# The head of a linear-attention and Mish kernel laid out anew, three q chunks loaded in runs of eight rows, first states built in column tiles

## The chip, the cores and the metric

The kernel runs on one core of one Trainium2 chip. The metric is the device time of one execution in microseconds (us), lower is better; it is taken as the median of several runs. A profile is one further execution, recorded by the hardware profiler; its own time is given beside the runs.

The core has five engines with a queue each: PE (TensorE, matrix products; PEld are its weight loads), DVE (VectorE), ACT (ScalarE), POOL (GpSimd) and SP (SyncE, here used for DMA transposes). Each engine takes its instructions in the order in which the program issues them. Matrix products read the on-chip memory SBUF and write the accumulator memory PSUM, which DVE and ACT read.

## What is computed

Two stages with nothing between them but a change of layout. The first is a decaying linear attention, 4 batches, 8 heads, 768 positions, head size 64; the second is a matrix product, an activation h · tanh(softplus(h)) (called Mish on the chip) and a second matrix product, on the 3072 tokens of width 512 that the first stage gives.

```python
def _attn_ref(q, k, v, lam):                      # q, k, v: (4, 8, 768, 64)
    ...
    Dmask = np.where(rel >= 0, lam[:, None, None] ** rel[None, :, :], 0.0)
    lam_pow = lam[:, None, None] ** (pos[None, :, None] + 1)
    lam_block = lam ** block
    for b in range(nb):
        ...
        intra = np.einsum('bhic,bhjc->bhij', qb, kb) * Dmask[None]
        intra = np.einsum('bhij,bhjd->bhid', intra, vb)
        inter = np.einsum('bhid,bhde->bhie', qb * lam_pow[None], kv_state)
        out[:, :, sl] = intra + inter
        kb_dec = kb * rev_pow[None]
        kv_state = lam_block[None, :, None, None] * kv_state + np.einsum('bhsd,bhse->bhde', kb_dec, vb)
    return out

def _moe_ref(x, w_in, w_out):                     # (3072, 512), (512, 2048), (2048, 512)
    h = x @ w_in
    sp = np.where(h > 20.0, h, np.log1p(np.exp(np.minimum(h, 20.0))))
    g = h * np.tanh(sp)
    return (g @ w_out)
```

## The kernel before

**Tiling.** The 768 positions are cut into six groups n of 128 positions (the kernel uses blocks of 128, not the reference's 64). A chunk i = 4n + b is group n of batch b, with all 8 heads: 128 positions by 512. Group n has 4 chunks, thus 512 tokens.

**A chunk of groups 0 and 1** goes through three functions. `first_t` turns k and q on PE so that the head size lies on the partitions (four 128x128 transposes each, into the PSUM tiles `pk` and `pq`); ACT copies `pk` to `pkT` and DVE copies `pq` to `pqT`. `first_s` multiplies the two, eight products into two PSUM tiles `pS`, and DVE multiplies these with the decay table `dm` (group 0) or a triangle (group 1) into `sb`, two operations of 128x512. `first_o` multiplies `sb` with v into `pO`, eight products, for group 1 with four more that bring in the state of group 0; ACT copies `pO` to the chunk's columns of `xt`. Below, t(c), s(c) and o(c) stand for these three on chunk c.

**The second stage** takes `xt`. For group 0, `mm1_unit` u = 0 to 15 makes 128 of the 2048 hidden columns for all 512 tokens (four products of 512 columns into `ph`, of which there are two PSUM buffers) and ACT applies Mish into `hsg`. `mm1_part` does the first 384 tokens of such a unit ahead, when the fourth chunk is not there yet. For group 1, `mm1_tile` (c, s) makes a quarter of the hidden columns for one chunk (16 products of 128 columns). After that `mm2_unit` multiplies `hsg` with `w_out` (four products of 512 columns); from there on the steps of the attention for groups 2 to 5 (`pair_s`, `pair_o`, `pair_a`) are slipped in between the dense units at numbered places.

**The head** is the stretch until the units of group 0 run without a stop. PE also gets products of zeros there (`busy(m)`: m products of 512 columns), whose results nobody reads. The decays come from lam: its logarithm is spread over the partitions, and from it come `dm`, `lk`, `lq`, `lbc` and `lqt` by exponentials on ACT.

**States.** `state_step(0, b)` makes batch b's state after group 0: four 128x128 products of `ktil` (k scaled by `lk`, made by `scale_k`) with v into a PSUM tile `pv`, of which only the 64x64 blocks on the diagonal are wanted; DVE multiplies with `lbm`, which holds the decay there and zero elsewhere, into `w`. `state_step(1, b)` adds `w` on DVE and scales on POOL into `wcp`, eight small POOL operations in all. `group_state` does the same for later groups, with products of 64 columns into two halves of the partitions (column tiles), two chunks to a PSUM tile.

**What sets the order.** The schedule is written by hand: every engine runs its instructions in the order of the source. POOL is at once an engine and the queue that issues nearly all loads, also in source order: k, q and v of a chunk in 128 partitions times 8 heads of 256 bytes, the weights in rows of up to 2 KB. A load on POOL can wait for a free semaphore, that is for the load eight places before it to land; what stands behind it on POOL waits too. SP issues the DMA transposes of the later groups (`turn`: `qraw` and `kraw`), each after POOL has scaled the chunk's k.

## Time and profile before

| | us |
|---|---|
| three runs, median (lowest to highest) | 212.15 (211.38 to 212.17) |
| the profiled execution, its own time | 213.28 |
| its span, first to last instruction | 211.5 |
| PE / DVE / ACT / POOL busy in it | 203.1 / 69.3 / 86.3 / 102.4 |

The profiled execution took 1.1 us more than the median; 1.8 us of its time lie outside the span. Times in the views count from the start of the span. A row of the timeline merges neighbouring instructions of one kind: start, time until the last of them has ended, engine, line, what is written and read, how many, and in brackets how long the engine had been idle and what ended that. A product's end includes its way through the array, so the next row of PE can start before the row's end; the step from start to start tells how fast PE goes on.

### The profile page before, as it was taken

The page shows a single profiled execution, that of the slowest core. Times are in us where ns is not written, and L with a number is a line of the kernel's source. Part 1 is how long each engine was busy: PE and PEld are TensorE (multiplying, and loading weights), DVE is VectorE, ACT ScalarE, POOL GpSimd, SP SyncE. Part 2 cuts the span into 40 slices and gives each one's busy share as a digit, 9 for nine tenths or more (in the row PEclk, how much of TensorE's full clock was granted, in tenths as well). Part 3 has the DMA queues.
Part 4 walks back from the last instruction along what each step waited for, and adds up shares of the span by engine and source line. Part 5 has one row for each costly group of instructions (what it writes and reads, how often), then busy time and mean ns, then how long its engine had stood idle before and what let it go on. Part 6 is the DMA issues. An engine that isn't in the chain of part 4 may idle for free.

```text
span 211.5 us, 4241 instructions
## 1 busy us (share of the span) xinstructions
PE 203.1 (96%) x1728; PEld 110.2 (52%) x1728; DVE 69.3 (33%) x131; ACT 86.3 (41%) x146; POOL 102.4 (48%) x149
## 2 busy tenths in 40 slices
PE   7798999999997999999999999999999999999994
PEld 2465546999644544455544454544445544444442
DVE  6867746650004442042440042582042600000000
ACT  5664566656321111356412356312456221566120
POOL 7997379948992558796965076931000000000000
PEclk9999999999999999999999999999999999999999
DMA  9999999999999999999996999996902032100112
GB/s 132 132 159 172 192 145 115 152 195 168 114 146 209 195 179 177 171 188 148 149 161 152 190 81 84 144 167 152 183 1 51 3 99 99 51 3 0 50 50 99
DMA packets 109894, 26.76 MB, mean 127 GB/s; under 512 B 102578, under 2 KB 106930, under 8 KB 109874
## 3 DMA queue, kind: packets, MB, share of 16 engines
q0 software_dynamic: 78080, 13.37, 91.8%
q1 hardware_dynamic: 27296, 6.63, 20.4%
q10 hardware_dynamic: 4498, 6.49, 9.9%
q8 instruction: 13, 0.21, 0.5%
q14 instruction: 7, 0.06, 0.1%
HBM read 27.26 MB, written 6.29 MB: 159 GB/s over the span
## 4 chain that ended last, share of the span: by engine, by line
PE 75%; POOL 13%; DMA 9%; issue 1%; DVE 0%; POOLq 0%
PE po L431 35%; PE ph L399 27%; DMA kn<-in_k_dram 6%; PE ph L417 5%; DMA kraw<-ktil 3%; POOL vz L79 3%; POOL ktil L266 3%; POOL qn L76 2%; POOL kn L68 2%; PE pS L343 2%; PE pO L370 2%; POOL win L92 1%; POOL win L95 1%; PE pv L319 1%; PE pO L349 1%
## 5 line engine op out<-in xcount | busy, mean ns | idle before, releaser
L431 PE MATMUL po<-wout,hsg 128*128 128x512 f16 (+2 forms) x400 | 85.4, 371 | 0.0
L399 PE MATMUL ph<-xt,win 128*128 128x512 f16 (+2 forms) x332 | 73.5, 371 | 0.4 <-ACT hsg L406 0.2
L406 ACT ACTIVATE hsg<-ph 128x512 f16<-128x512 f32 x80 | 47.5, 597 | 30.2 <-PE ph L399 29.8
L431 PEld LDWEIGHTS <-hsg 128*128 128x128 f16 x400 | 37.8, 98 | 42.3
L399 PEld LDWEIGHTS <-win 128*128 128x128 f16 x332 | 30.9, 98 | 34.7 <-issue 1.5
L446 ACT ACTIVATE osb<-po 128x512 f32<-128x512 f32 (+1 forms) x24 | 14.2, 593 | 75.4 <-PE po L431 70.6
L358 DVE TENSOR_TENSOR sb<-pS,maskT 128x512 f16<-128x512 f32 x32 | 20.0, 683 | 64.0 <-PE pS L343 64.0
L68 POOL DMA_DIRECT2D kn<-in_k_dram x23 | 20.9, 909 | 5.3 <-issue 1.9
L79 POOL DMA_DIRECT2D vz<-in_v_dram x24 | 21.6, 905 | 2.7 <-DMA win<-in_moe_w_in_dram 2.0
...
L266 POOL TENSOR_TENSOR ktil<-kn,lk 128x512 f16<-128x512 f16 x16 | 16.6, 1050 | 3.0 <-ACT hsg L406 2.9
L376 DVE TENSOR_TENSOR xtok<-pO,lqt 128x512 f16<-128x512 f32 x16 | 10.3, 686 | 16.8 <-PE pO L370 16.8
L417 PE MATMUL ph<-xt,win 128*128 128x128 f16 x256 | 15.3, 219 | 0.0
L417 PEld LDWEIGHTS <-win 128*128 128x128 f16 x256 | 14.5, 98 | 0.1
L440 DVE COPY osb<-po 128x128 f32<-128x128 f32 x1 | 0.3, 290 | 38.7 <-PE po L431 38.7
L421 ACT ACTIVATE hsg<-ph 128x512 f16<-128x512 f32 x16 | 9.6, 597 | 6.9 <-PE ph L417 6.9
L387 POOL COPY tick<-hsg 1x1 f16<-1x1 f16 x25 | 4.4, 176 | 12.2 <-ACT hsg L406 12.1
L324 POOL TENSOR_TENSOR wc<-raws,lbc 128x512 f16<-128x512 f32 x6 | 6.6, 1113 | 5.5 <-DVE raws L323 5.5
L163 PE MATMUL busy<-kzero 128*128 128x512 f16 x18 | 7.6, 516 | 1.2 <-DVE kzero L149 1.2
L266 DVE TENSOR_TENSOR ktil<-kn,lk 128x512 f16<-128x512 f16 (+1 forms) x8 | 6.6, 846 | 0.0
L241 DVE TENSOR_TENSOR sb<-pS,maskT 128x512 f16<-128x512 f32 x8 | 5.2, 686 | 4.2 <-PE pS L237 4.2
L343 PE MATMUL pS<-qraw,kraw 64*128 64x128 f16 x128 | 5.1, 218 | 1.2 <-DMA kraw<-ktil 1.2
...
## 6 DMA issues: line engine op xcount, KB each, us to landing
...
```

Of the source, the lines that this page charges most:

```text
L68: nc.gpsimd.dma_start(out=kn[i], in_=chunk_rows(k, i))
L76: nc.gpsimd.dma_start(out=qn[i], in_=chunk_rows(q, i))
L79: nc.gpsimd.dma_start(out=vz[i % NVB][:, :, 0:D], in_=chunk_rows(v, i))
L266: (nc.vector if i < B or i >= (NG - 1) * B else nc.gpsimd).tensor_tensor(out=t, in0=kn[i], in1=bc(lk, 2, D), op=ALU.mult)
L358: nc.vector.tensor_tensor(out=s.sb[x][t], in0=pS[x][t], in1=bc(maskT, 1, JP), op=ALU.mult)
L376: nc.vector.tensor_tensor(out=xtok[:, :, :, t, :], in0=s.pO[t], in1=bc(bc(lqj[:, :, t], 1, 2), 3, D), op=ALU.mult)
L399: nc.tensor.matmul(ph_t[ni][:, lo:hi], win_t(ni, kc), xt[n][:, kc, lo:hi], start=(kc == 0), stop=(kc == NKC - 1))
L406: nc.scalar.activation(hsg[n][:, ni, :], ph_t.pop(ni), AF.Mish)
L417: nc.tensor.matmul(ph[:, u, :], win_t(w * s + u, kc), xt[n][:, kc, b * C : (b + 1) * C], start=(kc == 0), stop=(kc == NKC - 1),)
L421: nc.scalar.activation(hsg[n][:, w * s : w * s + w, b * C : (b + 1) * C], ph, AF.Mish)
L431: nc.tensor.matmul(po[:, lo:hi], hsg[n][:, ki, b * C : (b + 1) * C], wout[part][:, kk, lo:hi], start=(ki == 0), stop=(ki == NKI - 1),)
L446: nc.scalar.activation(o, i, AF.Copy)
```

## The change

- **q of chunks 1 to 3** is loaded with eight neighbouring positions of one head to a partition: 128 runs of 2 KB in place of 1024 runs of 256 bytes, into tiles of their own. Their turn on PE is 16 ordinary products with parts of the identity as the moving operand (64 columns each, into one or the other half of the partitions of a PSUM tile in f32) in place of four transposes into f16.
- **States of groups 0 and 1** come from `state_half`, the form in column tiles that later groups had: 16 products of 64 columns for two chunks. Group 0's go straight into the diagonal blocks of one tile `wst`, which DVE has cleared beforehand, by two DVE operations on 64 partitions each; `lbm` and its making are gone. Group 1's sum needs two DVE operations and one of POOL for each half. Group 0's are made after units 1 and 3 (before: after units 3, 5, 7 and 9), group 1's after tiles (6,1) and (6,2) (before: between (4,1) and (5,0)).
- **Decays.** The logarithm for pairs of heads (`lnp`) comes from two small products of its own instead of copies; `lq` from four ACT operations instead of one on DVE and one on ACT. Both halves of `dm`'s arguments are made before q of chunk 0 is cast.
- **Zero products.** Two stand between the turns of k and q of chunk 0; in all 16 in place of 18.
- **The end of the head.** s(3) now stands before o(2), and only units 0 and 1 have a part made ahead (before: units 0, 1 and 2). `scale_k(1)` is done before the units, `scale_k(2)` and `scale_k(3)` after unit 1.
- **Group 1's steps** each lie later among the units and tiles: t(4) after unit 12 (11), s(4) after 14 (13), t(5) and o(4) after 15, then tile (4,0) directly.
- **POOL's queue.** `scale_k(6)` stands ahead of the load of v of chunk 7.
- **The first pair steps** among the dense units of groups 0 and 1 stand at 11, 14 and 17 in place of 9, 13 and 16.

At the end of the head, PE's queue was this before (L217 the turn of chunk 3's q, L256 its o(2), L163 a zero product, L237 s(3), L399 the part of unit 0; a row for the weights and one for the product, repeats left out):

```order
L217 LDWEIGHTS qn
L217 MATMUL pq<-ident,qn 128x128
...
L256 LDWEIGHTS vz_71
L256 MATMUL pO<-sb,vz_71 128x128
...
L163 LDWEIGHTS kzero
L163 MATMUL busy<-kzero 128x512
L237 LDWEIGHTS pkT
L237 MATMUL pS<-pqT,pkT 128x128
...
L399 LDWEIGHTS win_77
L399 MATMUL ph<-xt,win_77 128x384
```

It is this now (L225 the new turn of q, L252 s(3), L271 o(2), L176 a zero product, L398 the part of unit 0):

```order
L225 LDWEIGHTS qn_119
L225 MATMUL pq<-ident,qn_119 64x64
L252 LDWEIGHTS pkT
L252 MATMUL pS<-pqT,pkT 128x128
...
L271 LDWEIGHTS vz_71
L271 MATMUL pO<-sb,vz_71 128x128
...
L176 LDWEIGHTS kzero
L176 MATMUL busy<-kzero 128x512
...
L398 LDWEIGHTS win_77
L398 MATMUL ph<-xt,win_77 128x384
```

o(2) moved behind s(3); the part of unit 0, which reads what o(2) gives, stays behind both.

DVE's queue around the first states, before (L266 scales k, L299 makes the state of one batch in two operations):

```order
L266 TENSOR_TENSOR ktil<-kn,lk 128x512
L299 TENSOR_TENSOR w_158<-pv,lbm 128x256
L299 TENSOR_TENSOR w_159<-pv,lbm 128x256
L266 TENSOR_TENSOR ktil<-kn,lk 128x512
L299 TENSOR_TENSOR w_160<-pv,lbm 128x256
L299 TENSOR_TENSOR w_161<-pv,lbm 128x256
```

And now (L281 scales k, L313 makes the state of two batches in two operations, one for each half of the partitions):

```order
L281 TENSOR_TENSOR ktil<-kn_98,lk 128x512
L281 TENSOR_TENSOR ktil<-kn,lk 128x512
L313 TENSOR_TENSOR wst<-pv,lbc 64x8x64 x2
L281 TENSOR_TENSOR ktil<-kn,lk 128x512 x2
L313 TENSOR_TENSOR wst<-pv,lbc 64x8x64 x2
```

The scaling of k of chunks 2 and 3 now stands behind the first half's states, one after the other.

PE's queue ahead of the first tile of group 1, before (L256 the last products of o(4), L237 s(5), L217 t(6), L417 tile (4,0)):

```order
L256 LDWEIGHTS vz_73
L256 MATMUL pO<-sb,vz_73 128x128
L237 LDWEIGHTS pkT
L237 MATMUL pS<-pqT,pkT 128x128
...
L217 LDWEIGHTS qn
L217 MATMUL pq<-ident,qn 128x128
L417 LDWEIGHTS win_77
L417 MATMUL ph<-xt,win_77 128x128
```

And now (L267 and L271 o(4), L416 tile (4,0)):

```order
L267 LDWEIGHTS wst
L267 MATMUL pO<-pqT,wst 128x128
L271 LDWEIGHTS vz_73
L271 MATMUL pO<-sb,vz_73 128x128
...
L416 LDWEIGHTS win_77
L416 MATMUL ph<-xt,win_77 128x128
```

s(5) and t(6) no longer stand between o(4) and the tile that reads its result.

The diff, cut to its core:

```diff
+        if i < B:
+            qn[i] = const.tile([128, RS, D], F16, name=f"qn{i}")
+            n, b = divmod(i, B)
+            nc.gpsimd.dma_start(
+                out=qn[i].rearrange("p r c -> p (r c)"),
+                in_=q[b, :, n * C : (n + 1) * C, :].rearrange("h (s r) c -> h s (r c)", r=RS))
...
+    half = const.tile([1, 2, 128], F32, name="half")
+    nc.vector.memset(half, 0.0)
+    for t in range(2):
+        nc.vector.memset(half[:, t, 64 * t : 64 * t + 64], 1.0)
...
     nc.tensor.matmul(lamb, one1, lam1, start=True, stop=True)
-    busy(3)
+    lamp = ps.tile([128, JP], F32, name="lamp", tag="pS")
+    for t in range(2):
+        nc.tensor.matmul(lamp, half[:, t, :], lam1.rearrange("p (j t) -> p j t", t=2)[:, :, t],
+                         start=(t == 0), stop=(t == 1))
+    busy(1)
...
     def q_decays():
-        nc.scalar.activation(lq, lq, AF.Exp)
-        nc.scalar.activation(lqt, lnb, AF.Exp, scale=eq)
-
-
-    lbm = const.tile([128, JP, 128], F32, name="lbm")
-
+        for j in range(JP):
+            nc.scalar.activation(lq[:, j, :], ei, AF.Exp, scale=lnp[:, j : j + 1])
+
+    own = ident.rearrange("p (j x s) -> p j x s", j=JP, x=2)
...
-    def first_t(c):
+    def first_t(c, m=0):
 
         out_ = []
         first = c < B
         for src, name in ((k0 if c == 0 else kn[c] if first else ktil[c], "pk"),
                           (q0 if c == 0 else qn[c], "pq")):
-            pt = ps.tile([128, JP, C], F16, name=name, tag=name)
-            for j in range(JP):
-                nc.tensor.matmul(
-                    pt[:, j, :], src[:, 2 * j : 2 * j + 2, :].rearrange("p h c -> p (h c)"), ident,
-                    is_transpose=True, start=(j == 0), stop=(j == JP - 1),
-                )
+            if 0 < c < B and name == "pq":
+                pt = ps.tile([128, JP, C], F32, name=name, tag=name)
+                for r in range(RS):
+                    for x in range(2):
+                        nc.tensor.matmul(
+                            pt[64 * x : 64 * x + 64].rearrange("p j (s r) -> p j s r", r=RS)[:, :, :, r],
+                            src[:, r, :], own[:, :, x, :], start=True, stop=True)
+            else:
+                pt = ps.tile([128, JP, C], F16, name=name, tag=name)
+                for j in range(JP):
+                    nc.tensor.matmul(
+                        pt[:, j, :], src[:, 2 * j : 2 * j + 2, :].rearrange("p h c -> p (h c)"), ident,
+                        is_transpose=True, start=(j == 0), stop=(j == JP - 1),
+                    )
             out_.append(work.tile([128, JP, C], F16, name=f"{name}T", tag=f"{name}T", bufs=2))
             if name == "pk":
                 nc.scalar.activation(out_[-1], pt, AF.Copy)
+                busy(m)
...
-    def state_step(n, b, spare):
-
-        i = n * B + b
-        pv = ps.tile([128, JP, 128], F32, name="pv", tag=spare, bufs=2)
-        for j in range(JP):
-            nc.tensor.matmul(
-                pv[:, j, :].rearrange("p (a e) -> p a e", a=2),
-                ktil[i][:, 2 * j : 2 * j + 2, :].rearrange("p h c -> p (h c)"),
-                vz[i % NVB][:, 2 * j : 2 * j + 2, 0:D], start=True, stop=True,
-            )
-        if n:
-            raw = work.tile([128, JP, 128], F32, name="raw", tag="raw", bufs=4)
-        for hf in range(2):
-            hs = slice(2 * hf, 2 * hf + 2)
-            if n == 0:
+    def state_half(n, h, spare, bufs=2):
+
+        pv = ps.tile([128, 2, JP, D], F32, name="pv", tag=spare, bufs=bufs)
+        for x in range(2):
+            i = n * B + 2 * h + x
+            for j in range(JP):
+                for t in range(2):
+                    nc.tensor.matmul(
+                        pv[64 * t : 64 * t + 64, x, j, :], ktil[i][:, 2 * j + t, :],
+                        vz[i % NVB][:, 2 * j + t, 0:D], start=True, stop=True)
+        rows = [slice(64 * t, 64 * t + 64) for t in range(2)]
+        own = [wst[rs, 2 * h : 2 * h + 2, :, rs] for rs in rows]
+        if n == 0:
+            for rs, o in zip(rows, own):
                 nc.vector.tensor_tensor(
-                    out=wst[b][hf], in0=pv[:, hs, :], in1=lbm[:, hs, :], op=ALU.mult)
-            else:
-                nc.vector.tensor_tensor(
-                    out=raw[:, hs, :], in0=pv[:, hs, :], in1=wst[b][hf], op=ALU.add)
-        if n:
-            for t in range(2):
-                rs = slice(64 * t, 64 * t + 64)
-                nc.gpsimd.tensor_tensor(
-                    out=wcp[b // 2][0][rs, b % 2, :, :], in0=raw[rs, :, rs],
-                    in1=bc(lbc[rs, :], 2, D), op=ALU.mult)
-
...
+                    out=o, in0=pv[rs], in1=bc(bc(lbc[rs, :], 1, 2), 3, D), op=ALU.mult)
+            return
+        raw = work.tile([128, 2, JP, D], F32, name="raws", tag="raws", bufs=2)
+        if n == 1:
+            for rs, o in zip(rows, own):
+                nc.vector.tensor_tensor(out=raw[rs], in0=pv[rs], in1=o, op=ALU.add)
+        else:
             nc.vector.tensor_tensor(out=raw, in0=pv, in1=wcp[h][n % 2], op=ALU.add)
-            nc.gpsimd.tensor_tensor(
-                out=wcp[h][(n + 1) % 2], in0=raw, in1=bc(bc(lbc, 1, 2), 3, D), op=ALU.mult)
+        nc.gpsimd.tensor_tensor(
+            out=wcp[h][(n + 1) % 2], in0=raw, in1=bc(bc(lbc, 1, 2), 3, D), op=ALU.mult)
 
     def pair_a(s):
         if s.n < NG - 1:
-            group_state(s.n, s.spare)
+            for h in range(2):
+                state_half(s.n, h, s.spare)
...
+    def clear(b):
+        nc.vector.memset(wst[:, b], 0.0)
+
     nc.scalar.activation(k0, kn[0], AF.Copy)
+    nc.scalar.activation(lnp, lamp, AF.Ln)
     decays(0)
-    pair_decays()
+    decays(1)
     nc.vector.tensor_copy(q0, qn[0])
     nc.scalar.activation(dm[:, 0], dm[:, 0], AF.Exp)
-    decays(1)
-    first_t(0)
+    first_t(0, 2)
+    clear(0)
     nc.scalar.activation(dm[:, 1], dm[:, 1], AF.Exp)
-    q_arguments()
+    nc.scalar.activation(lk, lnb, AF.Exp, scale=ek)
+    nc.scalar.activation(lqt, lnb, AF.Exp, scale=eq)
+    nc.scalar.activation(lbc, lnp, AF.Exp, scale=float(C))
     busy(1)
     first_s(0)
-    nc.scalar.activation(lk, lnb, AF.Exp, scale=ek)
-    nc.scalar.activation(lbc, lnp, AF.Exp, scale=float(C))
+    first_t(1)
+    clear(1)
     q_decays()
-    busy(2)
-    first_t(1)
-    nc.scalar.preload_act_table(AF.Mish)
     busy(1)
+    first_o(0)
     first_s(1)
-    first_o(0)
     busy(3)
     first_t(2)
-    busy(1)
+    clear(2)
+    nc.scalar.preload_act_table(AF.Mish)
+    first_o(1)
     first_s(2)
-    first_o(1)
     busy(3)
     first_t(3)
+    clear(3)
+    first_s(3)
     first_o(2)
-    busy(1)
-    first_s(3)
+    busy(2)
     mm1_part(0, 0, 0, GT - C)
     first_o(3)
     mm1_part(0, 1, 0, GT - C)
-    mm1_part(0, 2, 0, GT - C)
     scale_k(0)
-    nc.vector.memset(lbm, 0.0)
-    for hp in range(2):
-        rs = slice(64 * hp, 64 * hp + 64)
-        nc.vector.tensor_copy(lbm[rs, :, rs], bc(lbc[rs, :], 2, D))
+    scale_k(1)
...
     scale_k(B + 1)
     load_q(NVB - 1)
+    scale_k(B + 2)
     load_v(NVB - 1)
...
-    steps = {11: ((first_t, 4),), 13: ((first_s, 4),), 14: ((first_t, 5),),
-             15: ((first_o, 4), (first_s, 5), (first_t, 6))}
+    steps = {12: ((first_t, 4),), 14: ((first_s, 4),), 15: ((first_t, 5), (first_o, 4))}
     for u in range(NKI):
         mm1_unit(0, u)
-        if u in (3, 5, 7, 9):
-            state_step(0, (u - 3) // 2, "po")
-        if u in (1, 3, 5):
-            scale_k((u + 1) // 2)
+        if u in (1, 3):
+            state_half(0, u // 2, "po")
+        if u == 1:
+            scale_k(2)
+            scale_k(3)
...
-    steps = {(4, 0): ((first_o, 5), (first_s, 6)), (4, 1): ((first_t, 7), (state_step, 0)),
-             (4, 2): ((first_o, 6), (first_s, 7), (state_step, 1)), (4, 3): ((state_step, 2),),
-             (5, 0): ((first_o, 7), (state_step, 3))}
+    steps = {(4, 0): ((first_s, 5), (first_t, 6)), (4, 1): ((first_o, 5), (first_s, 6)),
+             (4, 2): ((first_t, 7),), (4, 3): ((first_o, 6), (first_s, 7)), (5, 0): ((first_o, 7),),
+             (6, 1): ((state_half, 0),), (6, 2): ((state_half, 1),)}
     for c in range(B, 2 * B):
         for s in range(WS):
             mm1_tile(c, s)
             for f, i in steps.get((c, s), ()):
-                f(*((1, i, "po") if f is state_step else (i,)))
+                f(*((1, i, "po") if f is state_half else (i,)))
...
-            steps = (((9, pair_s, 0), (13, pair_o, 0), (16, pair_s, 1), (20, pair_o, 1),
+            steps = (((11, pair_s, 0), (14, pair_o, 0), (17, pair_s, 1), (20, pair_o, 1),
                       (24, pair_a, 1)) if n < NT else
```

29 lines of the change are left out of this document (6 added, 23 removed).

## The prediction

> **What bounds the kernel.** I read the page's busy times and chain first, then the timeline of the first 25 us, then the rows at which PE stands still.
>
> ```profile
> PE 203.1 (96%) x1728; PEld 110.2 (52%) x1728; DVE 69.3 (33%) x131; ACT 86.3 (41%) x146; POOL 102.4 (48%) x149
> PE 75%; POOL 13%; DMA 9%; issue 1%; DVE 0%; POOLq 0%
> ```
>
> PE is busy 203.1 of 211.5 us and carries 75% of the chain. Whatever delays PE anywhere stays to the end; whatever leaves PE alone is worth nothing. PE has room in the head and at a few waits. The head:
>
> ```profile
> 3.10 1.46 PE L163 MATMUL busy<-kzero 128*128 128x512 f16 x3
> 3.42 1.14 DVE L182 SCALAR_TENSOR_TENSOR dm<-rel,lnb,gone 128x128 f32<-128x128 f32 x4 [0.39 <-ACT lnb L171]
> 5.26 0.64 DVE L470 CAST q<-qn 128x512 f16<-128x512 f32 x1 [0.33 <-DMA qn<-in_q_dram]
> 5.96 0.61 PE L217 MATMUL pq<-ident,q 128*128 128x128 f16 x4 [0.70 <-DVE q L470]
> 6.86 0.41 DVE L225 COPY pqT<-pq 128x512 f16<-128x512 f16 x1
> 7.33 0.61 PE L237 MATMUL pS<-pqT,pkT 64*128 64x128 f16 x8 [0.34 <-DVE pqT L225]
> 8.02 1.29 DVE L241 TENSOR_TENSOR sb<-pS,dm 128x512 f16<-128x512 f32 x2
> 10.27 0.61 PE L237 MATMUL pS<-pqT,pkT 64*128 64x128 f16 x8
> 10.82 0.75 PE L256 MATMUL pO<-sb,vz 128*128 128x128 f16 x8
> 10.89 1.29 DVE L241 TENSOR_TENSOR sb<-pS,dm 128x512 f16<-128x512 f32 x2 [0.67 <-PE pS L237]
> 11.40 0.81 PE L163 MATMUL busy<-kzero 128*128 128x512 f16 x3
> 13.18 0.40 PE L237 MATMUL pS<-pqT,pkT 64*128 64x128 f16 x8 [0.31 <-ACT pkT L223]
> 13.62 1.29 DVE L241 TENSOR_TENSOR sb<-pS,dm 128x512 f16<-128x512 f32 x2 [0.50 <-PE pS L237]
> 15.71 0.60 ACT L258 ACTIVATE xt<-pO 128x512 f16<-128x512 f32 x1
> 15.82 0.40 PE L237 MATMUL pS<-pqT,pkT 64*128 64x128 f16 x8
> 16.25 1.29 DVE L241 TENSOR_TENSOR sb<-pS,dm 128x512 f16<-128x512 f32 x2 [0.56 <-PE pS L237]
> 16.36 0.81 PE L399 MATMUL ph<-xt,win 128*128 128x384 f16 x4
> 17.60 0.55 PE L256 MATMUL pO<-sb,vz 128*128 128x128 f16 x7 [0.37 <-DVE sb L241]
> 17.98 2.13 PE L399 MATMUL ph<-xt,win 128*128 128x384 f16 x20
> 18.18 0.60 ACT L258 ACTIVATE xt<-pO 128x512 f16<-128x512 f32 x1 [1.88 <-PE pO L256]
> 19.71 2.31 ACT L406 ACTIVATE hsg<-ph 128x512 f16<-128x512 f32 x4 [0.93 <-PE ph L399]
> 20.36 1.02 PE L399 MATMUL ph<-xt,win 128*128 128x512 f16 x4 [0.24 <-ACT hsg L406]
> 21.22 0.39 PE L289 MATMUL pv<-vz,ktil 128*128 128x128 f16 x4
> 21.64 0.75 DVE L299 TENSOR_TENSOR w<-pv,lbm 128x256 f16<-128x256 f32 x2 [1.08 <-PE pv L289]
> 22.31 0.68 DVE L266 TENSOR_TENSOR ktil<-kn,lk 128x512 f16<-128x512 f16 x1
> ```
>
> What to see: three zero products take 1.46 us at 3.10 and 0.81 at 11.40, so PE runs at half speed until about 11 us. With some 0.17 us for the way through the array, a product of 512 columns steps by 0.43 slow and 0.215 fast, one of 128 columns by 0.107 and 0.054 (the seven at 17.60 take 0.38 to the next row). The chunks follow each other as a ring: scores on PE, `sb` on DVE, the next chunk's turns, copies, scores; `sb` starts at 8.02, 10.89, 13.62 and 16.25. From 20.36 the units run without a stop: that is the mark I carry forward.
>
> **The change, part by part.**
>
> *Chunk 0.* DVE now makes all eight decay arguments first: 3.42 + 8 x 0.285 = 5.70, and only then casts q, whose data were in by 5.26. The turn of q follows 0.70 later (5.26 to 5.96), at 6.40, is through 0.61 later, and is copied at 7.05 (the copy at 6.86 had itself waited for the second four decays). So s(0) comes at 7.52 (7.33) and `sb` at 8.21 (8.02). The two products of lam and the two zero products fall into time in which PE waits for k and q: nothing, in place of the trio at 3.10.
>
> *Chunk 1.* PE now has s(0), turns, one zero product, o(0), s(1). o(0) can start 1.35 after `sb` (16.25 to 17.60), at 9.56, and takes 8 x 0.107 = 0.86 slow; with 0.1 for the change of shape s(1) stands at 10.5 (10.27), `sb` at 11.1 (10.89).
>
> *q's turn.* The nearest operation is the state product of 64 columns into halves of the partitions:
>
> ```profile
> 80.67 0.69 PE L319 MATMUL pv<-vz,ktil 128*64 128x64 f16 x32
> ```
>
> Less 0.2 for its last one's way, 32 step by 0.016. Bounds for the new 16: 0.26 by this row, 0.86 if each costs as much as a fast product of 128 columns. I take 0.26 (half the columns, both halves used in turn; 0.5 slow) and 0.1 for the change of shape. The copy from f32 PSUM is bounded by 0.41 (the f16 copy) and 0.68 (512 columns on DVE at 22.31); f32 has four bytes to read, so I take 0.68. Clearing `wst` (four memsets) lies behind each copy, while PE makes the scores: nothing, 0.25 a chunk without that cover.
>
> *Chunks 2 and 3.* PE's path from scores to scores: scores 0.33 (13.18 to the next row), three zero products 0.65, k 0.22, q 0.36, 0.25 to the copy, copy and hand-over 0.73: 2.54. DVE's: 0.44 to `sb` (13.18 to 13.62), 1.22 for the pair less its tail, 0.73: 2.39, shorter. Before it was 2.91 and 2.64. With 0.1 of slow clock left, s(2) at 13.1, s(3) at 15.65, `sb` of chunk 3 at 16.1: **0.15 gained** on 16.25.
>
> *The end of the head.* o(2) is now queued behind s(3): 15.65 + 0.33 to 16.42, through at 16.6. Its copy to `xt` takes 0.60: 17.3. The part of unit 0 reads that and starts at 17.3 (16.36). o(3) follows at 17.95, its copy ends at 19.2 (18.78); the part of unit 1 lies under it. Unit 0's rest and Mish at 19.65 (19.71). Unit 2 now has nothing made ahead and no third buffer: it waits for Mish, 0.65 after that (19.71 to 20.36), 20.3, with the first half of the states (0.1 + 0.26) inside the wait. Unit 3 at 21.17 instead of 20.36: **+0.81**.
>
> *States of group 0.* Before: four times 0.22 on PE behind unit 3. Now one half behind it, 0.26 + 0.2 for two changes of shape. But DVE has four operations of 512 columns between the halves' products: states of the first half (two on 64 partitions: I take 0.62 each, since a pair of 256 columns takes 0.75 and one of 512 takes 0.68), then k of chunks 2 and 3. From 20.3 that ends at 22.85; PE is there at 22.3 and waits 0.6. Unit 4 at 23.1 (21.45), with 0.66 of old state work no longer ahead: the balance is **+1.0**.
>
> *Group 1.* These waits were there:
>
> ```profile
> 31.71 1.04 PE L399 MATMUL ph<-xt,win 128*128 128x512 f16 x4
> 32.81 0.40 PE L217 MATMUL pk<-ident,ktil 128*128 128x128 f16 x4
> 34.90 0.40 PE L237 MATMUL pS<-pqT,pkT 64*128 64x128 f16 x8
> 35.00 0.60 ACT L258 ACTIVATE xt<-pO 128x512 f16<-128x512 f32 x1
> 35.62 0.40 PE L217 MATMUL pk<-ident,ktil 128*128 128x128 f16 x4 [0.33 <-POOL ktil L266]
> 41.73 1.29 DVE L241 TENSOR_TENSOR sb<-pS,maskT 128x512 f16<-128x512 f32 x2 [0.76 <-PE pS L237]
> 41.87 1.06 PE L417 MATMUL ph<-xt,win 128*128 128x128 f16 x16
> 43.08 0.38 PE L289 MATMUL pv<-vz,ktil 128*128 128x128 f16 x4 [0.15 <-DVE sb L241]
> ```
>
> From start to start, less the products' own steps: 0.23 before 32.81, 0.49 before 35.62 (both for POOL's k), 0.33 before 43.08: 1.05. All go, since the turns now come 2 us and more later than POOL's k. That is also why the shorter q loads are booked at nothing: no row of the head waits for q of chunks 1 to 3, and what they free in POOL's queue reaches group 1's k, which is no longer waited for. What is late next: tile (4,0) stands right behind o(4) and needs its copy: 0.2 + 0.60 + 0.05 = 0.85 (s(5) and t(6) covered it). o(7) stands one tile (0.89, 16 products) behind s(7), whose `sb` is done 0.43 + 1.29 later; its third product waits 0.45. Together 1.30: **+0.25**. States of group 1: two halves of 0.46 for four times 0.22, +0.04.
>
> *The stall at 65.*
>
> ```profile
> 52.97 0.94 POOL L68 DMA_DIRECT2D kn<-in_k_dram  x1
> 54.91 8.80 PE L431 MATMUL po<-wout,hsg 128*128 128x512 f16 x40
> 65.23 0.23 PEld L343 LDWEIGHTS <-kraw 64*128 64x128 f16 x8 [1.36 <-DMA kraw<-ktil]
> ```
>
> PE waits 1.36 for k of chunk 9 from a DMA transpose. `pair_s` now comes two units (8 x 0.215 = 1.72) later, and the dense units start 1.29 later (1.0 + 0.25 + 0.04): PE wants it at 66.9. It will be late too: the chain behind it runs over POOL, which first scales group 1's states.
>
> ```profile
> L324 POOL TENSOR_TENSOR wc<-raws,lbc 128x512 f16<-128x512 f32 x6 | 6.6, 1113 | 5.5 <-DVE raws L323 5.5
> ```
>
> The second half's products end five tiles before the dense units, 56.2 - 4.45 = 51.75; 0.2, 1.29 on DVE and 1.11 on POOL make 54.4 for the load that stood at 52.97, and shift the landing from 65.2 to 66.65. **-1.36**, with 0.25 to spare. From there on PE has the same work as before.
>
> **Sum.** +1.0 + 0.25 + 0.04 - 1.36 = -0.07: against the profiled 213.28 that is 213.2. Moved by the 1.1 us by which the profile exceeds the runs: 212.15 - 0.07, **212.1**. A measurement here tells about 0.5% (1.06 us) from no change.
>
> **The rivals.**
>
> *The clock opens earlier (faster).* The rows at 5.96 and 7.33 show PE idle for 0.70 and 0.34 before the stretch that ended the half speed. The two zero products fill most of the first gap; q's later cast leaves some 0.45 and 0.27. If full speed comes at about 7.7, o(0) and two score steps lose 0.7: -0.8, 211.4; if the waits at the head's end come out shorter by as much as I have rounded up (0.7), 210.7. The Trainium skill ("TensorE: Matmul & The Clock Gate", Part 1) has the clock open after one busy window of about 3.4 us of a window that runs freely; by that rule this case is decided by where the window lies. The trace agrees in that it took more than one stretch of that length, and no row shows the window.
>
> *q's turns cost like full products (slower).* Place: PE's path in chunks 1 to 3. 48 products at 0.054 instead of 0.016 put up to 1.8 on it, of which chunk 1 hides some behind `sb`: about +1.4, 213.5. It decides from 0.022 a product more on. For it: they write PSUM in steps of eight elements, which no row shows; against: 80.67. The Trainium skill ("TensorEngine Tiling (Array Packing)", Restrictions and Gotchas) says that column tiles shut off the fast weight load, and by the clock-gate page's figure for weight loads 64 columns would take 53 ns, an estimate that gives this rival's time; the row's 16 ns disagree.
>
> *The stall comes back (slower).* If POOL's chain slips by more than the 0.25 to spare, each further us is a us: up to +1.3, 213.4. The change would then only have moved the wait.
>
> **Chances.** Forecast 0.42, the earlier clock 0.22, that with a shorter end of the head 0.10, dear turns 0.14, the stall 0.12. The forecast's own range is 0.8 to either side. Of the earlier clock a third lies beyond -1.06, of the two slow cases two thirds beyond +1.06: faster 0.22, same 0.56, slower 0.22. The range 211.0 to 213.5 leaves out the second fast case and the ends of the slow ones.
>
> **What would show it.** Right: the trio of zero products before chunk 3's turns at 0.81; a PE gap before the 384-column products near 17; one before the second state half near 22 ended by DVE; one before the first tile ended by ACT's `xt`; no gap at `kraw`. Wrong: units running at full rate before 20.5 us, turns of q longer than 0.6 us, or a gap over 0.5 us at `kraw`.

## The result and the profile after

| | us, median (lowest to highest) | ratio to before, 95% interval |
|---|---|---|
| before, six runs | 211.59 (210.88 to 212.17) | |
| after, six runs | 217.22 (215.76 to 218.54) | 1.0255, 1.021 to 1.030 |
| after, the profiled execution | 217.08, span 215.3 | |

A ratio, here and among the experiments, compares executions of both kernels that were measured together, without those that ran disturbed; a median is of all executions of a kernel.

Slower by 2.5%, far above the predicted 212.1 and outside its range (211.0 to 213.5). The page of after, its busy times, granted clock and chain by line:

```profile
PE 204.9 (95%) x1794; PEld 111.2 (52%) x1794; DVE 68.6 (32%) x124; ACT 86.7 (40%) x150; POOL 99.1 (46%) x143
...
PEclk9999999999999969999999999999999999999999
...
PE po L430 36%; PE ph L398 32%; PE ph L416 6%; DMA kraw<-ktil 5%; PE pS L342 2%; DMA kn<-in_k_dram 2%; PE pv L306 2%; PE pO L369 2%; PE pS L252 1%; PE pO L271 1%; DVE pqT L240 1%; PE busy L176 1%; PE pk L231 1%; PE pO L348 1%; DVE sb L256 1%
```

The page of before, its granted clock and chain by line:

```profile
PEclk9999999999999999999999999999999999999999
...
PE po L431 35%; PE ph L399 27%; DMA kn<-in_k_dram 6%; PE ph L417 5%; DMA kraw<-ktil 3%; POOL vz L79 3%; POOL ktil L266 3%; POOL qn L76 2%; POOL kn L68 2%; PE pS L343 2%; PE pO L370 2%; POOL win L92 1%; POOL win L95 1%; PE pv L319 1%; PE pO L349 1%
```

PE is busy 1.8 us more than before in a span that is 3.8 us longer, and in one of the 40 slices the granted clock of PE falls to 6 tenths; before, all 40 showed 9. In the chain, the DMA that brings `kraw` has grown from 3% to 5%. Both point to one place in PE's timeline of after (L342 are the scores of `pair_s`):

```profile
66.42 0.62 PE L342 MATMUL pS<-qraw,kraw 64*128 64x128 f16 x16
...
72.96 0.40 PE L342 MATMUL pS<-qraw,kraw 64*128 64x128 f16 x8
75.81 0.61 PE L342 MATMUL pS<-qraw,kraw 64*128 64x128 f16 x8 [2.45 <-DMA kraw<-ktil]
```

The first pair (chunks 8 and 9) is asked for at 66.42 and gets its 16 products at once: the wait at 65 of the profile before is gone, as predicted. The second pair (L342 again, six units later) gets chunk 10's eight products at 72.96 and then stands until 75.81. With 0.23 for the eight products that is a wait of 2.62 us, for `kraw` of chunk 11. The chain of waits of that stretch names the transfer:

```profile
65.54 10.22 DMA kraw<-ktil
```

It was issued at 65.54 and took 10.22 us to land. What follows the wait is shown by the stretches view (length; busy us and instructions of PE, PEld, DVE, ACT and POOL; then the granted clock, the DMA share and GB/s):

```profile
75.80:79.20 3.40, 3.39 (x31) 1.81 (x32) 1.29 (x2) 0.00 (x0) 0.00 (x0) 0.55 1.65 203
```

For the 3.4 us behind the wait PE has 0.55 of its clock. In the six runs the mean clock is 0.992 in four (217.08 to 218.54) and 1.000 in two (215.76 and 215.95).

The head and group 1 in PE's timeline of after, the rows that answer to those quoted of before:

```profile
7.28 0.40 PE L252 MATMUL pS<-pqT,pkT 64*128 64x128 f16 x8
...
10.04 0.82 PE L176 MATMUL busy<-kzero 128*128 128x512 f16 x3
...
11.01 0.64 PE L225 MATMUL pq<-ident,qn 128*64 128x64 f16 x16
11.58 0.62 PE L271 MATMUL pO<-sb,vz 128*128 128x128 f16 x8
...
16.80 0.81 PE L398 MATMUL ph<-xt,win 128*128 128x384 f16 x4 [0.25 <-ACT xt L273]
...
22.00 0.32 PE L306 MATMUL pv<-vz,ktil 128*64 128x64 f16 x8 [0.31 <-DVE ktil L281]
22.61 0.32 PE L306 MATMUL pv<-vz,ktil 128*64 128x64 f16 x8 [0.29 <-DVE ktil L281]
22.85 7.94 PE L398 MATMUL ph<-xt,win 128*128 128x512 f16 x36
...
36.08 1.05 PE L416 MATMUL ph<-xt,win 128*128 128x128 f16 x16 [0.69 <-ACT xt L273]
...
44.63 0.22 PE L271 MATMUL pO<-sb,vz 128*128 128x128 f16 x1 [0.27 <-DVE sb L256]
...
49.74 0.44 PE L306 MATMUL pv<-vz,ktil 128*64 128x64 f16 x16
50.12 1.07 PE L416 MATMUL ph<-xt,win 128*128 128x128 f16 x16
...
55.96 1.24 PE L430 MATMUL po<-wout,hsg 128*128 128x512 f16 x5
```

The dense units (L430) start at 55.96; before, L431 started at 54.91.

### The profile page after: what moved, and what is told of

The parts are those of the page before. It is cut to its first block, busy times and chain, and to the rows that moved or that the text cites. A ratio compares the mean times of both kernels' runs of the same rounds, so it can differ in the third digit from the quotient of the medians.

```text
span 215.3 us, 4362 instructions
## 1 busy us (share of the span) xinstructions
PE 204.9 (95%) x1794; PEld 111.2 (52%) x1794; DVE 68.6 (32%) x124; ACT 86.7 (40%) x150; POOL 99.1 (46%) x143
## 4 chain that ended last, share of the span: by engine, by line
PE 87%; DMA 6%; DVE 3%; issue 1%; ACT 1%; DVEq 0%
PE po L430 36%; PE ph L398 32%; PE ph L416 6%; DMA kraw<-ktil 5%; PE pS L342 2%; DMA kn<-in_k_dram 2%; PE pv L306 2%; PE pO L369 2%; PE pS L252 1%; PE pO L271 1%; DVE pqT L240 1%; PE busy L176 1%; PE pk L231 1%; PE pO L348 1%; DVE sb L256 1%
## 5 line engine op out<-in xcount | busy, mean ns | idle before, releaser
L430 PE MATMUL po<-wout,hsg 128*128 128x512 f16 (+2 forms) x400 | 86.4, 374 | 0.0
L398 PE MATMUL ph<-xt,win 128*128 128x512 f16 (+2 forms) x328 | 73.1, 374 | 0.5 <-ACT xt L273 0.3
L430 PEld LDWEIGHTS <-hsg 128*128 128x128 f16 x400 | 38.0, 98 | 43.1 <-issue 1.4
L398 PEld LDWEIGHTS <-win 128*128 128x128 f16 x328 | 30.8, 98 | 36.3 <-issue 2.0
L85 POOL DMA_DIRECT2D qn<-in_q_dram x20 | 18.0, 900 | 1.9 <-issue 1.4
L281 POOL TENSOR_TENSOR ktil<-kn,lk 128x512 f16<-128x512 f16 x16 | 16.7, 1054 | 3.1 <-DMA kn<-in_k_dram 3.0
L416 PE MATMUL ph<-xt,win 128*128 128x128 f16 x256 | 15.6, 219 | 0.7 <-ACT xt L273 0.7
L416 PEld LDWEIGHTS <-win 128*128 128x128 f16 x256 | 14.5, 98 | 1.1 <-issue 0.8
L322 POOL TENSOR_TENSOR wc<-raws,lbc 128x512 f16<-128x512 f32 x8 | 8.6, 1097 | 13.7 <-DVE raws L319 8.5
L342 PE MATMUL pS<-qraw,kraw 64*128 64x128 f16 x128 | 5.4, 223 | 2.5 <-DMA kraw<-ktil 2.5
L176 PE MATMUL busy<-kzero 128*128 128x512 f16 x16 | 6.4, 489 | 1.2 <-DVE kzero L158 1.2
L342 PEld LDWEIGHTS <-kraw 64*128 64x128 f16 x128 | 3.7, 96 | 6.0 <-issue 3.4
L256 DVE TENSOR_TENSOR sb<-pS,maskT 128x512 f16<-128x512 f32 x8 | 5.2, 687 | 5.1 <-PE pS L252 5.1
```

Source lines behind the costliest of these rows:

```text
L85: nc.gpsimd.dma_start(out=qn[i], in_=chunk_rows(q, i))
L281: (nc.vector if i < B or i >= (NG - 1) * B else nc.gpsimd).tensor_tensor(out=t, in0=kn[i], in1=bc(lk, 2, D), op=ALU.mult)
L342: nc.tensor.matmul(pS[x][t][:, j, :], kraw[i][rows[t], j, :], qraw[i][rows[t], j, :], start=True, stop=True)
L398: nc.tensor.matmul(ph_t[ni][:, lo:hi], win_t(ni, kc), xt[n][:, kc, lo:hi], start=(kc == 0), stop=(kc == NKC - 1))
L416: nc.tensor.matmul(ph[:, u, :], win_t(w * s + u, kc), xt[n][:, kc, b * C : (b + 1) * C], start=(kc == 0), stop=(kc == NKC - 1),)
L430: nc.tensor.matmul(po[:, lo:hi], hsg[n][:, ki, b * C : (b + 1) * C], wout[part][:, kk, lo:hi], start=(ki == 0), stop=(ki == NKI - 1),)
```

## The experiments

Two theories were to be told apart, and two smaller rivals. **T**: the transfers decide. Group 1's states come 6 us and more later on PE (49.7 and 51.1 us; before, between 39.4 and 45.1); POOL's scaling of them (`wc`) stands in POOL's queue ahead of the load of chunk 11 and of the scaling of chunks 8 to 11, so their turns on SP start late and land among other transfers. **P**: the new places of the pair steps are what costs. **H**: the head and group 1 are the whole loss. **B**: a fetch of instructions holds the transfers up. A theory **C** came out of the first four runs: the loads of group 3 crowd the turns out.

| run | us, median | ratio to before, 95% interval |
|---|---|---|
| old pair places | 215.32 | 1.0156, 1.0126 to 1.0186 |
| second pair late | 218.25 | 1.0286, 1.0250 to 1.0323 |
| states early | 212.94 | 1.0046, 1.0027 to 1.0066 |
| filled gap | 215.88 | 1.0181, 1.0155 to 1.0207 |
| before, once more | 211.62 | 1.0005, 0.9973 to 1.0036 |
| loads later | 213.51 | 1.0087, 1.0054 to 1.0120 |
| states early and order | 211.04 | 0.9970, 0.9950 to 0.9991 |
| states early, q by heads | 211.78 | 1.0001, 0.9975 to 1.0028 |
| all three edits | 210.81 | 0.9959, 0.9936 to 0.9981 |
| before, states late | 213.09 | 1.0049, 1.0025 to 1.0073 |
| all three, old pair places | 211.31 | 0.9960, 0.9937 to 0.9984 |
| before, new pair places | 211.87 | 0.9976, 0.9944 to 1.0008 |

**1. The pair steps back at their old places** (in the changed kernel)

```diff
-            steps = (((11, pair_s, 0), (14, pair_o, 0), (17, pair_s, 1), (20, pair_o, 1),
+            steps = (((9, pair_s, 0), (13, pair_o, 0), (16, pair_s, 1), (20, pair_o, 1),
```

> Only the four places of the pair steps are set back to 9, 13, 16 and 20; everything else is the changed kernel. Theory T (the transfers decide: GpSimd makes the first states' copies of group 1 eight places later in the program, so its loads of chunk 11 and its scaling of chunks 8 to 11 come about 1 us later, the turns fall among the other transfers, and kraw of chunk 11 lands at about 75.8 whatever asks for it): PE waits twice, about 1.2 for kraw of chunk 9 (asked for near 64.7, landing 65.9) and about 2.5 for kraw of chunk 11, and after the landing there is one unit of 0.88 us more to do, so about 217 to 218.5 us, not faster than the changed kernel. Rival P (the new places of the pair steps are what costs): back to about 213 us, kraw of chunk 11 landing near 72.

Neither theory had it: 215.32, with two short waits in PE's timeline of this run.

```profile
65.91 0.40 PE L342 MATMUL pS<-qraw,kraw 64*128 64x128 f16 x8 [0.45 <-DMA kraw<-ktil]
...
73.99 0.40 PE L342 MATMUL pS<-qraw,kraw 64*128 64x128 f16 x8 [0.50 <-DMA kraw<-ktil]
```

The wait for chunk 9 is there as T said (shorter), but chunk 11 landed at 74.0, not at 75.8. So the landing does depend on the places, and setting them back won 1.9 us, though not by the way that P meant: with `pair_s` later, the outputs of the dense units come earlier, and POOL, which holds the loads of chunk 13 back for such an output, issued them in after at 67.71 and here at 69.60 (POOL's timelines). Chunk 11's turn, issued at 65.54 and 66.34, is on its way both times, but in after the loads meet it nearer its start. That became theory C.

**2. The second pair asked for later**

```diff
-            steps = (((11, pair_s, 0), (14, pair_o, 0), (17, pair_s, 1), (20, pair_o, 1),
+            steps = (((11, pair_s, 0), (14, pair_o, 0), (20, pair_s, 1), (23, pair_o, 1),
```

> The scores of the second pair of group 2 are made behind unit 20 instead of 17, its values behind 23 instead of 20; the rest is the changed kernel. Theory T: kraw of chunk 11 still lands at about 75.8, but is asked for at about 75.6, so the wait of 2.5 us goes to 0.3 or less, and with it the stretch of half clock behind it (3.4 us long, about 1.5 us lost): 217.2 - 2.3 - 1.4 = about 213.5 us, mean clock 1.000. Rival B (an instruction fetch delays the transfers wherever they are): kraw lands later again and a wait over 1 us stays, 215 us or more. If the half clock has nothing to do with the wait, it stays and the time is about 215.

PE's timeline of this run, at its longest wait:

```profile
91.86 4.35 PE L398 MATMUL ph<-xt,win 128*128 128x512 f16 x13 [4.30 <-DMA xt<-xtok]
```

The stretch behind it (columns as above):

```profile
91.80:95.20 3.40, 3.34 (x10) 1.26 (x11) 0.00 (x0) 0.63 (x2) 0.69 (x2) 0.57 1.49 182
```

The step went as T said: `kraw` of chunk 11 landed at 75.8 again, was asked for at 75.90, and nothing waited for it. B expected a wait there, and none came; whether a fetch lengthens the way of the transfer is taken up at run 12. The time did not go as T said: `pair_o` at unit 23 gives its result three units later in the program, the last transpose into `xt` is issued at 82.53 and takes 9.20 us to land (5.2 in after), and the unit that reads it waits 4.30 us at 91.86. Behind that wait the clock is 0.57 for 3.4 us again. Here the late transfer was not waited out by moving only the step that asks first: what hangs on that step came late in its turn.

**3. Group 1's states early**

```diff
-             (4, 2): ((first_t, 7),), (4, 3): ((first_o, 6), (first_s, 7)), (5, 0): ((first_o, 7),),
-             (6, 1): ((state_half, 0),), (6, 2): ((state_half, 1),)}
+             (4, 2): ((first_t, 7),), (4, 3): ((first_o, 6), (first_s, 7), (state_half, 0)),
+             (5, 0): ((first_o, 7),), (5, 1): ((state_half, 1),)}
```

> The two halves of group 1's states are made behind tiles (4,3) and (5,1) instead of (6,1) and (6,2), about 8 us earlier; the rest is the changed kernel. Theory T: GpSimd's copies are done about 8 us earlier, its load of chunk 11's k is issued near 47 instead of 54.1, the turns of chunks 8 to 11 have landed before 70, no wait at kraw of chunk 9 or 11 and no half clock behind it: 217.2 - 2.6 - 1.5 = about 213.1 us; if the units also start no later than 56, down to 212.7. Rival P (places of the pair steps) and rival H (the longer head and group 1 are the whole loss): no more than 0.5 us gained.

212.94 against 213.1 expected: 4.3 of the 5.6 us are gone with two entries of a table, and P and H, which allowed at most 0.5, fall as the main cause. The view of the tile `kraw` gives, for the one turn of the stretch from 61 to 77 us that the trace can follow (chunk 11's), the time from issue to landing, 10.2 in after. With the states early:

```profile
DMA to landing us min/median/max: 5.0/5.0/5.0
```

Issued at 61.19, it landed at 66.2, where PE asks at 72.6.

**4. The gap filled with products of zeros**

```diff
+            if i == 11:
+                for _ in range(8):
+                    nc.tensor.matmul(pS[x][0].rearrange("p j c -> p (j c)"), kzero, kzero2,
+                                     start=True, stop=True)
```

> Eight products of zeros (128x512 each, some 0.22 us at full rate, 1.8 in all) are put between the scores of chunk 10 and those of chunk 11, into a bank that the scores overwrite; the rest is the changed kernel. If the idle time of PE is what brings the half clock, the gap is filled down to about 0.8 us, no half clock follows, and the time falls by what it cost: about 215.7 us, mean clock 1.000. If the half clock comes by itself (a throttle of another kind), it stays: 217.2 us. Under both, kraw of chunk 11 lands at about 75.8.

PE's timeline of this run, from chunk 11's scores (L346) to the next values (L373):

```profile
75.72 0.40 PE L346 MATMUL pS<-qraw,kraw 64*128 64x128 f16 x8 [0.28 <-DMA kraw<-ktil]
...
78.88 0.63 PE L373 MATMUL pO<-vz,sb 128*128 128x64 f16 x16
```

The same stretch as in after, in this run:

```profile
75.80:79.20 3.40, 3.40 (x47) 1.93 (x48) 1.29 (x2) 0.60 (x1) 0.18 (x1) 1.00 1.65 209
```

And the values in PE's timeline of after:

```profile
80.38 0.63 PE L369 MATMUL pO<-vz,sb 128*128 128x64 f16 x16
```

`kraw` landed at 75.7 as before, and the clock stayed at 1.00. From the scores to the values it takes 78.88 - 75.72 = 3.16 us, in after 80.38 - 75.81 = 4.57: the half clock costs **1.41 us**, and it is PE's idle time that brings it. The medians say 1.34. The mean clock is 1.000 in all five executions of this run; in after it was 0.992 in four of six.

**5. The kernel before, once more**

> The kernel before, unchanged, profiled once more. If the wait of 1.36 us for kraw of chunk 9 belongs to every execution, it is there again, with a span near 211.5. If it was a chance of the one execution that was profiled (its own time was 1.7 us above the median of the runs), the span is near 209.9 and the gap is under 0.4 us: then the changed kernel had nothing to win there.

PE's timeline of this run, the first dense units and the scores of both pairs:

```profile
54.73 8.80 PE L431 MATMUL po<-wout,hsg 128*128 128x512 f16 x40
63.46 0.62 PE L343 MATMUL pS<-qraw,kraw 64*128 64x128 f16 x16
...
70.86 0.62 PE L343 MATMUL pS<-qraw,kraw 64*128 64x128 f16 x16
```

The span is 210.0 and nothing waits for `kraw`: all 16 products run at once both times. So the wait of 1.36 us in the first profile does not come in every execution, and the median of the six runs (211.59, less 1.8 outside the span: 209.8) fits executions without it. POOL's timeline in that first profile:

```profile
46.72 0.87 POOL L76 DMA_DIRECT2D qn<-in_q_dram  x1 [1.91 <-DMA wout<-in_moe_w_out_dram]
...
52.97 0.94 POOL L68 DMA_DIRECT2D kn<-in_k_dram  x1
```

POOL's timeline in this run:

```profile
45.34 5.43 POOL L307 TENSOR_TENSOR wc<-raw,lbc 64x256 f16<-64x256 f32 x8
50.72 0.94 POOL L68 DMA_DIRECT2D kn<-in_k_dram  x1
```

There POOL had stood 1.91 us until a part of `w_out` had landed, and came to the load of chunk 11 2.25 us later than here. POOL's timeline of after:

```profile
51.77 1.04 POOL L322 TENSOR_TENSOR wc<-raws,lbc 128x512 f16<-128x512 f32 x1 [8.21 <-DVE raws L319]
...
54.10 0.95 POOL L70 DMA_DIRECT2D kn<-in_k_dram  x1
```

It comes there 3.38 us later than in this run of before, after 8.21 us of standing still for the sums of the state.

**6. The loads of group 3 four units later** (in the changed kernel)

```diff
-                    u = 7 + x // 2 * 4
+                    u = 11 + x // 2 * 4
```

> The loads of group 3 (chunks 12 to 15) are issued four units later (behind units 11, 15, 19, ... instead of 7, 11, 15, ...); the rest is the changed kernel. Theory C (the loads of chunks 12 and 13 share the DMA engines with the turns and put off kraw of chunk 11): it lands near 73, the wait of 2.5 us and the half clock go almost wholly: about 213.5 us, if no later chunk is then late. Rival G (only the time at which GpSimd comes to the scaling of chunks 8 to 11 decides): kraw of chunk 11, issued at 65.5 as before, still lands after 75, and the time stays within 0.7 of 217.2.

213.51 against 213.5 by C; G falls. Chunk 11's turn was issued at 66.34, not at 65.5 as expected, and still landed at 73.2. Its way, from issue to landing by the view of the tile, is in this run:

```profile
DMA to landing us min/median/max: 6.9/6.9/6.9
```

In before once more, by SP's timeline and the same view:

```profile
62.91 1.29 SPq L275 DMA_TRANSPOSE kraw<-ktil  x1
...
DMA to landing us min/median/max: 6.1/6.1/6.1
```

So chunk 11 is 6.7 us late in after (75.76 against 69.03) for two reasons: issued 2.6 later (65.54 against 62.91), which is POOL's queue, and 4.1 longer on the way (10.2 against 6.1), of which 3.3 go when the loads of group 3 come later, so that the turn meets chunk 12's first (67.48); in after it meets chunk 13's (67.71) with chunk 12's right ahead of it (63.97 and 64.84). How the loads do it this run does not tell (see run 12). Either cure, run 3 or this one, takes the long wait away, since it brings the landing to the request or ahead of it.

**7. States early, and two waits of the change taken away**

```diff
-    scale_k(0)
-    scale_k(1)
+    for i in range(B):
+        scale_k(i)
...
-    steps = {12: ((first_t, 4),), 14: ((first_s, 4),), 15: ((first_t, 5), (first_o, 4))}
+    steps = {11: ((first_t, 4),), 13: ((first_s, 4),), 14: ((first_t, 5), (first_o, 4)),
+             15: ((first_s, 5),)}
...
-    steps = {(4, 0): ((first_s, 5), (first_t, 6)), (4, 1): ((first_o, 5), (first_s, 6)),
+    steps = {(4, 0): ((first_t, 6),), (4, 1): ((first_o, 5), (first_s, 6)),
```

(`scale_k` of chunks 2 and 3 is taken out behind unit 1.)

> On top of the early states of group 1: k of chunks 2 and 3 is scaled right behind that of chunks 0 and 1, ahead of the first states; and the turns, scores and values of chunks 4 and 5 are set so that a unit stands between the values of chunk 4 and the first tile. The waits named in the prediction, 0.6 for k at the second half of the states and 0.85 for xt of chunk 4, should go, with no new wait over 0.3: the dense units start near 54.2 instead of 55.6, and 212.9 falls to about 211.5 us, under the kernel before by some 0.5 us. If the waits only move to other places (pqT of chunk 4, scores of chunk 5), 212.5 or more.

PE's timeline of this run:

```profile
21.70 0.44 PE L306 MATMUL pv<-vz,ktil 128*64 128x64 f16 x16
...
34.55 0.40 PE L252 MATMUL pS<-pqT,pkT 64*128 64x128 f16 x8
34.88 1.07 PE L416 MATMUL ph<-xt,win 128*128 128x128 f16 x16
```

The 16 products of the second state half (21.70) and the first tile (34.88) no longer wait; the dense units start at 53.87 instead of 55.61. 211.04 is 0.3% under the kernel before, with an interval that just excludes no change.

**8. States early, q of chunks 1 to 3 by heads again**

```diff
-            qn[i] = const.tile([128, RS, D], F16, name=f"qn{i}")
...
+            qn[i] = const.tile([128, H, D], F16, name=f"qn{i}")
+            nc.gpsimd.dma_start(out=qn[i], in_=chunk_rows(q, i))
...
-            if 0 < c < B and name == "pq":
+            if False:
```

> On top of the early states of group 1: q of chunks 1 to 3 is loaded by heads as k is and turned by four transposes into f16, as in the kernel before. In the head, DVE's copy of pq (0.69 from f32 against 0.42 from f16) and the products (0.57 against 0.22 to the next) are both on the way from scores to scores: up to 0.6 us less for each of chunks 2 and 3 and some for chunk 1, unless DVE's own round (copy, two times sb) or the arrival of k and q sets the pace. If q's turns cost what the rows say: the part of unit 0 starts near 15.8 instead of 16.9, and the time is about 211.9 us. If the data's arrival or ACT's copies take over: 212.5 to 212.9.

PE's timeline of this run, the turn of chunk 2's q and the part of unit 0:

```profile
10.75 0.39 PE L228 MATMUL pq<-ident,qn 128*128 128x128 f16 x4
10.97 0.89 PE L268 MATMUL pO<-sb,vz 128*128 128x128 f16 x8
...
15.69 0.81 PE L395 MATMUL ph<-xt,win 128*128 128x384 f16 x4 [0.25 <-ACT xt L270]
```

211.78: the new q costs 1.16 us by the medians of runs 3 and 8 (0.95 by their ratios), and the part of unit 0 starts at 15.69 instead of 16.92. The turn steps 0.22 to the next row (10.75 to 10.97) against 0.57 in after (11.01 to 11.58), DVE's copy takes 0.42 against 0.69.

**9. All three edits together**

> The early states of group 1, the new order of the scaling and of chunks 4 and 5, and q of chunks 1 to 3 loaded by heads and turned by transposes, all three together. The two gains lie one behind the other on PE (head before 17 us, waits at 22 and 36 us), so they should add: 211.04 - 1.16 = about 209.9 us, 0.8% under the kernel before. If the earlier head only lengthens a later wait (for w_in or for k of chunk 4), 210.6 or more.

210.81: the lowest median of all, but the 1.16 did not add; between this and run 7 the intervals tell nothing apart. The case named in the expectation as the other way came: the earlier head meets k of chunks 4 and 5 (PE's timeline of this run).

```profile
28.50 0.40 PE L228 MATMUL pk<-ident,ktil 128*128 128x128 f16 x4
...
32.22 0.40 PE L228 MATMUL pk<-ident,ktil 128*128 128x128 f16 x4
```

PE is 0.23 late at 28.50 and at 32.22, from start to start; POOL's scaling of the two chunks (27.41 and 31.09, 1.04 and 1.07 long) ends just before each. Besides, full clock came later in this execution than in that of run 8 (last section), and the part of unit 0 at 16.11 instead of 15.69.

**10. One part alone in the kernel before: its group 1 states late**

```diff
-    steps = {(4, 0): ((first_o, 5), (first_s, 6)), (4, 1): ((first_t, 7), (state_step, 0)),
-             (4, 2): ((first_o, 6), (first_s, 7), (state_step, 1)), (4, 3): ((state_step, 2),),
-             (5, 0): ((first_o, 7), (state_step, 3))}
+    steps = {(4, 0): ((first_o, 5), (first_s, 6)), (4, 1): ((first_t, 7),),
+             (4, 2): ((first_o, 6), (first_s, 7)), (5, 0): ((first_o, 7),),
+             (5, 3): ((state_step, 0),), (6, 0): ((state_step, 1),),
+             (6, 1): ((state_step, 2),), (6, 2): ((state_step, 3),)}
```

> The kernel before with one thing changed: the four state steps of group 1 are made behind tiles (5,3), (6,0), (6,1) and (6,2) instead of (4,1) to (5,0). Theory T: GpSimd's eight copies (5.4 us) then end near 54 instead of 50.7 as in the second profile of before, everything that stands behind them (load of chunk 11, scaling of chunks 8 to 11, their turns) is some 3.3 us later; kraw of chunk 9 lands near 65.2 where PE asks near 63.5, so a wait of about 1.8 us comes back, and kraw of chunk 11 may bring another: 213.5 to 216 us. Rivals P and H (the pair steps' places, the head): no more than 0.4 us off the kernel before, 211.7.

PE's timeline of this run at its wait:

```profile
65.09 0.40 PE L343 MATMUL pS<-qraw,kraw 64*128 64x128 f16 x8 [1.28 <-DMA kraw<-ktil]
```

The stretch behind it:

```profile
65.10:68.50 3.40, 3.40 (x38) 1.81 (x39) 1.32 (x3) 0.60 (x1) 0.18 (x1) 1.00 1.86 214
```

The wait for chunk 9 comes by this alone (`kraw` at 65.05, expected near 65.2), no second one: 213.09, a little under what was expected, and 1.3 us above the kernel before, measured together with it (211.79; 1.0 by the ratio). P and H allowed 0.4. The wait of 1.28 us leaves the clock at 1.00.

**11. All three edits, with the old pair places**

> The same as the run with all three edits, but with the pair steps of group 2 back at 9, 13, 16 and 20. With the states early, kraw of chunk 9 and of chunk 11 have landed (near 61 and 67) before either set of places asks for them (from 62 and 69 on). Theory T: within 0.4 us of the run with all three edits, about 209.9 us. Rival P (the new places cost or save by themselves): 0.6 us or more to one side.

PE's timeline of this run at its wait for chunk 11:

```profile
71.61 0.40 PE L339 MATMUL pS<-qraw,kraw 64*128 64x128 f16 x8 [1.34 <-DMA kraw<-ktil]
```

POOL's timeline of this run:

```profile
51.47 0.87 POOL L82 DMA_DIRECT2D qn<-in_q_dram  x1 [1.94 <-DMA wout<-in_moe_w_out_dram]
```

By the ratio the same, but the expectation that both had landed in time was wrong: here POOL had waited 1.94 us for `w_out`, `kraw` of chunk 11 landed at 71.6, and PE waited. Of the ten executions that its ratio keeps, two took over 213.2 us; with the new places none of eleven did.

**12. The new pair places alone in the kernel before**

> The kernel before with the four places of the pair steps set to 11, 14, 17 and 20, and nothing else. Theory T (the places only say how much time the turns have; what makes them late in the changed kernel is GpSimd's late copies): both pairs are asked for later than before (kraw of chunk 9 near 65.2, of chunk 11 near 71.7) and have landed (62 and 69 in the second profile of before, perhaps 1 later since the loads of chunk 13 start sooner): no wait over 0.4 us, 211.7 us within 0.4. Rival P (the new places cost by themselves, for instance since the loads of group 3 start sooner): 212.7 us or more, with a wait at kraw of chunk 11.

PE's timeline of this run, the scores of chunk 11:

```profile
72.36 0.40 PE L343 MATMUL pS<-qraw,kraw 64*128 64x128 f16 x8 [0.53 <-DMA kraw<-ktil]
```

The same time as before within the measurement: the new places cost nothing by themselves. A wait of 0.53 us at chunk 11 in the profiled execution is more than was expected.

This run also limits theory C. The load of chunk 13 in POOL's timeline, and the time from issue to landing of chunk 11's turn, which SP issued at 65.97:

```profile
66.17 0.88 POOL L68 DMA_DIRECT2D kn<-in_k_dram  x1 [0.27 <-issue]
...
DMA to landing us min/median/max: 6.3/6.3/6.3
```

The turn is as late as in after and has the loads of chunk 13 right behind it, yet it took 6.3 us and not 10.2. Two things are different in after: chunk 12's loads stand closer ahead of the turn (63.97 and 64.84; here 62.33 and 63.20), and one transfer of the queue `q8 instruction`, a fetch of instructions, falls on the way (between 71.0 and 71.5; here none does). In run 6 such a fetch falls on the way as well (between 69.5 and 70.0), and that turn took 6.9. So a fetch alone does not make 10.2, and moving the loads takes most of the excess away. Whether it takes loads close together, or loads and a fetch at once (theory B), no run separates.

## Why the prediction was wrong

Against the second profile of before (run 5, span 210.0, the one that agrees with the median of the runs), after's 215.3 adds up: dense units 1.23 later (55.96 against 54.73), wait 2.62, half clock 1.41, together 5.26 of 5.3.

- **Up to the dense units: the waits right, the sum in part by luck.** The prediction had +1.29 (1.0 + 0.25 + 0.04); +1.23 came (+1.05 against the first profile), with the next two points, of opposite sign, in it. The wait of 0.6 for `ktil` is 0.31 + 0.29 of idle time (22.00, 22.61; 0.92 from start to start, less the products' steps); that for `xt` ahead of the first tile, put at 0.85, is a gap of 0.85 (idle 0.69 in the row at 36.08); o(7)'s 0.45 is 0.43 (44.63). Unit 4 stands at 22.85 for 23.1. Run 7 took the first two away (0.92 + 0.85) and won 1.9 us. But two of the three waits credited in group 1, those for POOL's k (0.23 and 0.49; the second is 0.39, since scores step by 0.33 to the next row), are not in run 5 either: there unit 4 stands at 21.99, 0.54 later than in the first profile, and both turns follow without a gap (33.04, 35.44). With the 0.66 of old state work behind unit 4 taken off, as the prediction does, the cost up to unit 4 against run 5 is 0.20 (22.85 - 21.99 - 0.66) where 1.0 was predicted, and behind it 1.03 where 0.29 was; against the first profile it is 0.74 and 0.31.
- **The earlier clock** (a rival, 0.22) came: scores at 7.28 in 0.40 and three zero products at 10.04 in 0.82 are at full rate, so `sb` of chunk 3 stood at 15.58 (DVE's timeline) instead of 16.1.
- **q's turns: mis-sized.** 0.36 was taken within 0.26 to 0.86; it is 0.57 (0.036 a product). With the f32 copy, taken rightly at 0.68, the new q costs about 1 us as long as the head sets the time (run 8); with the rest in order POOL's k hides part of it (run 9).
- **The stall at 65, -1.36: wrong twice.** First, it was no property of the kernel: the profile stood 1.1 above the median of the runs, the prediction moved its sum by that 1.1 and still credited the wait. Run 5 is 1.5 shorter in span, and the wait of 1.36 is what it lacks. Secondly, the predicted slip was right (load of chunk 11 at 54.4, measured 54.10; landing of chunk 9 at 66.65, measured 65.9, ahead of PE at 66.42), but it was followed to chunk 9 only.
- **The step that failed** is the sentence "From there on PE has the same work as before". The same slip reaches chunk 11, two turns down the queue, where `pair_s(1)` came only one unit later; and its way was taken as unchanged, though the turn now fell among loads of group 3 that had not slipped with it (chunk 13's at 67.71; in run 5 at 67.36). In its place the runs show a wait of 2.62 us for chunk 11 and 1.41 us of half clock behind it; with the states early both are gone (run 3). The rival "the stall comes back" had the mechanism, but the price of one shifted wait (1.3) and the wrong chunk. None of the cases had the half clock.
- **Neither part alone makes the loss.** In the kernel before, late states cost 1.0 to 1.3 us (run 10) and the new places nothing (run 12). In the changed kernel early states win 4.3 (run 3) and the old places 1.9 (run 1). Both parts together were not tried in the kernel before.

The Trainium skill ("TensorE: Matmul & The Clock Gate", "HAM oscillation — how this bites in real kernels") warns of PE gaps over some 3.4 us. The trace agrees that a gap brings half clock for one stretch of that length, but not on the gap: 2.62 us sufficed.
